# Scores of tiles 0 and 1 of a head pair in one PSUM buffer, and a new order of the units of a round

## The chip, the cores and the metric

The kernel runs on one core of one Trainium2 chip. The metric is the device time of one execution in microseconds (us). TensorE is called PE here, VectorE DVE, ScalarE ACT, GpSimd POOL, and SP is the engine whose queue issues the DMAs. PE writes its results to PSUM, from which DVE and ACT read them. Each engine works through its own instructions in the order of the program, and waits on semaphores for the others.

## The reference

Three stages follow each other; the change lies in the first and touches the start of the second.

```python
# 1. attention, 4 batches x 8 heads, 576 tokens, head size 64
scores = scale * np.matmul(q, k.transpose(0, 1, 3, 2))
mask = block_i >= block_j                       # blocks of 64 tokens
scores = np.where(mask, scores, -1000000000.0)
scores = scores - np.max(scores, axis=-1, keepdims=True)
attn = np.exp(scores)
attn = attn / (np.sum(attn, axis=-1, keepdims=True) + 1e-09)
out = np.matmul(attn, v)
# 2. x: 2304 tokens x 512, from out
h = x @ w_in                                    # 512 x 2048
g = np.where(h >= 1, h, np.where(h <= -1, 0.0, (h + 1) ** 2 / 4))
x = g @ w_out
# 3. a mixture of 8 experts on 32 slots, with softmax over tokens and over slots
```

## The kernel before

Two heads make a pair, so attention is 16 pairs (4 batches, 4 pairs each). A pair's 576 query rows are cut into tiles of 128 rows: tiles 0 to 3 for each of the two heads, and tile 4, which holds the last 64 rows of both heads. The mask is block-triangular, so tile i needs the first 128(i+1) keys.

The work of a pair is cut into units, named by two letters and a number. `sc`i computes the scores of tile i on PE: three passes of split fp32 for both heads, and for tiles 0 to 3 two small matmuls with `low` and `one` that add a large negative number where the mask is false. `mx`i takes row maxima on DVE into the tile `negm`, `ex`i the exponentials on ACT, with row sums as a by-product. `rs` makes reciprocals of the sums on DVE, and `no`i multiplies the rows with them on POOL. `pt`j turns chunks of the result on PE into PSUM, `pc`j copies them to SBUF (j = 1 and 3 on DVE, the others on ACT). `pa` and `pb` multiply with v on PE, for tiles 2 to 4 and for tiles 0 and 1. `xh` and `xl` split the result into two fp32r parts: `xh` on ACT and `xl` on DVE for tokens below 1024, one copy on DVE for later tokens. `kh`, `kl`, `qh` and `ql` split k and q, `lk`, `lq`, `lv` load, and `w0`, `w1`, `w2` prepare columns of `w_in`. `hm` is one block of the first product of stage 2 (12 matmuls, 128x512 each), `ha` (ACT) and `ho` (DVE) its bend; eleven such blocks are computed during attention, one in each of the rounds 9 to 19 (the table `EARLY`).

The order is written out by hand in the table `PLAN`. A round runs through it once. The digit ahead of a unit says how many pairs back the unit works: in round r, `3sc4` computes the scores of tile 4 of pair r-3, `2sc3` those of tile 3 of pair r-2, `5pa` the output of pair r-5. There are 22 rounds; rounds 5 to 17 have all units of attention. Every engine takes its share of the list in this order, and waits come from the tiles the units share.

PSUM is held by three pools: `psc` has two buffers of [128, 2, 512] fp32 (two banks each) for scores, `ptr` three of one bank for transposes, for `pb` and for the blocks `h`, and `ppv` one for `pa`. A unit that takes a buffer waits until the readers of its former content are done. In the kernel before, a round takes five score buffers, in the order sc4, sc1, sc0, sc3, sc2, from the two of `psc` in turn. So sc4 waits for ex3 of the round before, sc1 for ex2, sc0 for ex4, sc3 for ex1, and sc2 for ex0.

Stage 2 and 3 (`Moe.run`) follow after the last round, with their own order.

Of the kernel before, what the change touches and what calls it, by code (L numbers as in the profile page):

```python
# [7 lines left out]
F32 = mybir.dt.float32  # L8
# [6 lines left out]
P = 128  # L15
# [21 lines left out]
class Pair:  # L37
# [68 lines left out]

    def sc(self, i):
        e, nc = self.e, self.nc
        sc = self.scs[i] = e.psc.tile([P, 2, 512], F32, tag="sc", name=f"sc{self.nm}{i}")
        if i == 4:  # L110
            for k, (qa, ka) in enumerate(((0, 0), (0, 1), (1, 0))):
                for u in range(2):
                    nc.tensor.matmul(sc[:, u, 0:288], self.QD[:, qa], self.K[:, ka, 288 * u:288 * u + 288],
                                     start=(k == 0), stop=(k == 2))
            return
        n = 128 * (i + 1)
        rows = slice(0, 64), slice(64, 128)
        for k, (qa, ka) in enumerate(((0, 0), (0, 1), (1, 0))):
            for h, r in enumerate(rows):
                nc.tensor.matmul(sc[:, h, 0:n], self.Q[r, qa, 128 * i:128 * i + 128], self.K[r, ka, 0:n],  # L120
                                 start=(k == 0), stop=False)
        for h, r in enumerate(rows):
            nc.tensor.matmul(sc[:, h, n - 64:n], e.low[r], e.one[r], start=False, stop=True)  # L123

    def block(self, i):
        for u, b in enumerate(self.TILES[i]):
# [18 lines left out]
    def ex(self, i):  # L145
        for b, sc, pr in self.block(i):
            self.nc.scalar.activation(pr, sc, AF.Exp, bias=self.negm[:, b:b + 1], accum_out=self.sums[:, b:b + 1])  # L147
# [66 lines left out]
    def xl(self, a):  # L214
        for hi, lo, src in self.xparts(a):
# [4 lines left out]


PLAN = """
3sc4 4pc2 4no1 1ho0 4pt4 3ex2 2qh 4pt5 4pc5 3sc1 4pc4 3rs0 3mx4 3mx1 5pa
3ex4 3ex1 2ql 5xh1 5pb 2w2 5xh0 3rs2 3no2 4pc3 3no3 5xl1 3sc0 2sc3
3pt0 3mx0 3no4 5xl0 3pt1 1kh 1lq 2mx3 3lv 3ex0 3rs1 3pc1 4pt6 2sc2 0hm0
2mx2 1w1 3pc0 4pc6 2ex3 0ha0 1kl 0lk 3pt2 3pt3 3no0 0w0
"""
EARLY = {(9, 0): (0, 0), (10, 0): (0, 1), (11, 0): (0, 2), (12, 0): (0, 3), (13, 0): (1, 0), (14, 0): (0, 4),
         (15, 0): (1, 1), (16, 0): (0, 5), (17, 0): (1, 2), (18, 0): (0, 6), (19, 0): (1, 3)}
# [12 lines left out]
def attention(e, tc, nb=4, wl=(1, 1 + 2 * READY)):  # L242
    nc = tc.nc
    e.ENG = ENG

    def copy(eng, dst, src):
        if eng == "A":
            nc.scalar.copy(dst, src)  # L248
        elif eng == "D":
            nc.vector.tensor_copy(dst, src)  # L250
        else:
            nc.gpsimd.tensor_scalar(out=dst, in0=src, scalar1=1.0, scalar2=1.0, op0=ALU.mult, op1=ALU.mult)
    e.copy = copy
    e.eng = lambda c: nc.vector if c == "D" else nc.gpsimd

    e.QD, e.pr, e.v_ = [], [], []
    for i in range(2):
        e.QD.append(e.apool.tile([P, 2, P], F32R, tag=f"QD{i}", bufs=1, name=f"QD{i}"))
        z = (nc.gpsimd, nc.vector)[i]
        z.memset(e.QD[i][0:64, :, 64:P].bitcast(F32), 0.0)  # L260
        z.memset(e.QD[i][64:P, :, 0:64].bitcast(F32), 0.0)
        e.pr.append([e.apool.tile([P, P * (b // 2 + 1)], F32, tag=f"pr{i}{b}", bufs=1, name=f"pr{i}{b}")
                     for b in range(9)])
        z.memset(e.pr[i][8][:, 576:640], 0.0)
        e.v_.append(e.apool.tile([P, 5, 2, 64], F32, tag=f"natv{i}", bufs=1, name=f"vn{i}"))
        z.memset(e.v_[i][64:P, 4], 0.0)
    e.low = e.apool.tile([P, P], mybir.dt.bfloat16, tag="low", bufs=1, name="low")
    e.one = e.apool.tile([P, 64], mybir.dt.bfloat16, tag="one", bufs=1, name="one")
    nc.vector.memset(e.low, 0.0)
    nc.vector.memset(e.one, 1.0)  # L270
    for h in (0, 64):
        nc.vector.memset(e.low[h:h + 1, 0:64], -2.0 ** 127)
    pairs = [Pair(e, nc, b, p) for b in range(nb) for p in range(4)]
    n = len(pairs)
    plan = [(it - int(u[0]), u[1:]) for it in range(n + 6) for u in PLAN.split()]
    plan = [(i, u) for i, u in plan if ((i, int(u[2:])) in EARLY if u[0] == "h" and u[1] in "moa" else
                                        0 <= i < n if u[0] != "w" else wl[0] <= i < wl[1])]
    fill = [(int(u[0]), u[1:]) for u in FILL.split()]
    assert sorted(fill) == sorted(plan[:len(fill)])
    for i, u in fill + plan[len(fill):]:  # L280
        if u[0] == "h":
            e.moe.early(u[1], *EARLY[i, int(u[2:])])
        elif u[0] != "w":
            pairs[i].step(u)
        else:
            t, c = (i - wl[0]) // 2, slice((i - wl[0]) % 2 * 256, (i - wl[0]) % 2 * 256 + 256)
            if u == "w0" and c.start == 0:
                e.moe.w_raw(t)
            elif u == "w1":
                e.moe.w_mul(t, c)  # L290
                e.moe.w_bits(t, c)
            elif u == "w2":
                e.moe.w_parts(t, c, e.ENG["w"])
# [14 lines left out]
class Moe:  # L308
# [207 lines left out]
            self.g[b, f] = self.new([P, a, n], F32, f"g{b}_{f}")  # L516
        return self.g[b, f // a * a][:, f % a]

    def h_unit(self, b, f, mid=()):
        e, nc = self.e, self.nc  # L520
        n = self.BLK[b][1]
        w = self.w[f].rearrange("p a (k c) -> p a k c", k=4)
        ph = self.ph[b, f] = e.ptr.tile([P, 512], F32, tag="tr", name=f"h{b}_{f}")
        m = 0
        for kk in range(4):
            for wi, xi in ((0, 0), (0, 1), (1, 0)):
                nc.tensor.matmul(ph[:, 0:n], w[:, wi, kk], self.x(b, kk, xi)[:, 0:n], start=(m == 0), stop=(m == 11))  # L527
                m += 1
            if kk == 2:
                for fn, *a in mid:  # L530
                    getattr(self, fn)(*a)
        if f == 15:
            self.drop_x(b)
        if b == 4:
            self.drop(f"w{f}")
# [23 lines left out]
        nc.vector.tensor_tensor(out=g, in0=ph, in1=g, op=ALU.max)  # L559

    def early(self, what, b, f):
        if what == "m":
            self.h_unit(b, f)
        elif what == "a":
            self.bend_act(b, f, "D")
        else:
            self.bend_max(b, f, "D")
# [547 lines left out]
def tile_attention_mixtures(ctx, tc, q, k, v, w_in, w_out, phi, w1, w2a, w2b, outa, outb):  # L1115
# [33 lines left out]
    with tc.tile_pool(name="att", bufs=1, reuse_waits="tile") as e.apool:  # L1149
        attention(e, tc)  # L1150
        nc.sync.dma_start(e.phi, phi.rearrange("(k p) s -> p k s", p=P))
# [53 lines left out]
```

## Time and profile before

| | us |
|---|---|
| median of 3 runs | 538.68 |
| the three runs | 538.38, 538.68, 539.71 |
| the profiled execution | 538.28 |
| its span, first to last instruction | 536.5 |
| attention, rounds 0 to 20, within the span | about 5 to 209 |

In the profile's first part PE is busy 507.3 us (95% of the span), DVE 343.0 (64%), ACT 322.4 (60%) and POOL 201.6 (38%). These shares mix stages: during attention all four compute engines are busy most of the time, later PE works nearly alone and the end waits for weights from HBM. The engine rows that follow are read by their start times: the step from one row to the next on PE is what a unit cost there, its own work and its wait together, because the duration of a row of several matmuls covers gaps between them.

### The profile page before, as it was taken

Reading aid. Unit: us, or ns where it says so; the run is one execution under the profiler, and the core shown is the slowest. Engines: PE = TensorE matmul, PEld = TensorE weight load, DVE = VectorE, ACT = ScalarE, POOL = GpSimd, SP = SyncE. Lnnn points to the kernel's source line nnn. Section 1 sums busy time; section 2 is a strip of 40 time slices with the busy share of each in tenths; the row PEclk is TensorE's granted clock in tenths of the full one; section 3 lists DMA queues with packets and bytes.
Section 4 is the critical chain, followed back from the end, with each engine's and each line's share of the span. In section 5 each row is a group of like instructions: output and inputs, shape, how many; then the busy total and the mean of one; then the engine's idle time right before and its main releaser. Section 6 shows DMA issues by size and latency. Waiting matters only on the chain.

```text
span 536.5 us, 11758 instructions
## 1 busy us (share of the span) xinstructions
PE 507.3 (95%) x4538; PEld 384.6 (72%) x4538; DVE 343.0 (64%) x676; ACT 322.4 (60%) x732; POOL 201.6 (38%) x259
## 2 busy tenths in 40 slices
PE   6899999999999989999989999899999999989994
PEld 5687777777777767878767887788767888643463
DVE  7799998888886734888998645823464343531242
ACT  5899987777777642667768878634334545231131
POOL 4888986767775430555552212500001000010000
PEclk9799999999999999999999999999999999999997
DMA  4444454323221135412146875322176496799997
GB/s 154 118 125 124 117 129 121 101 85 110 73 72 51 28 106 188 160 46 78 41 137 230 281 265 168 121 93 83 25 258 227 158 374 217 256 339 399 410 413 303
DMA packets 42711, 91.01 MB, mean 170 GB/s; under 512 B 8736, under 2 KB 18080, under 8 KB 42656
## 3 DMA queue, kind: packets, MB, share of 16 engines
q1 hardware_dynamic: 42656, 90.26, 49.6%
q8 instruction: 36, 0.59, 0.5%
q14 instruction: 19, 0.16, 0.1%
HBM read 74.51 MB, written 14.68 MB: 166 GB/s over the span
## 4 chain that ended last, share of the span: by engine, by line
PE 65%; DVE 14%; ACT 7%; DMA 5%; issue 3%; POOL 0%; SPq 0%; DVEq 0%; ACTq 0%; POOLq 0%
PE h L527 32%; PE gn L581 5%; PE om L184 4%; PE sc L120 4%; PE lt L593 3%; PE s L631 3%; PE eh L987 3%; DMA ew<-in_w2b_dram 3%; ACT pr L147 2%; DVE nm L142 2%; DVE wab L455 2%; DVE g L559 2%; DVE g L558 2%; ACT g L545 1%; PE om L189 1%
## 5 line engine op out<-in xcount | busy, mean ns | idle before, releaser
L527 PE MATMUL h<-xh,w 128*128 128x512 f32 (+1 forms) x384 | 115.6, 368 | 0.0
L158 POOL TENSOR_SCALAR pr<-pr,sm 128x384 f32<-128x384 f32 (+2 forms) x144 | 86.3, 617 | 38.4 <-DVE sm L153 14.0
L527 PE MATMUL h<-xt,w 128*128 128x512 f32 x384 | 91.6, 395 | 1.7 <-ACT PT L248 1.7
L558 DVE SCALAR_TENSOR_TENSOR g<-g 128x512 f32<-128x512 f32 (+1 forms) x52 | 37.4, 720 | 82.3 <-ACT g L545 81.7
L147 ACT ACTIVATE pr<-sc,nm 128x512 f32<-128x512 f32 (+2 forms) x144 | 78.6, 559 | 11.9 <-DVE nm L142 8.6
L527 PEld LDWEIGHTS h<-xt,w 128*128 128x128 f32 x384 | 70.5, 188 | 18.6 <-ACT PT L248 2.1
L527 PEld LDWEIGHTS h<-xh,w 128*128 128x128 f32 x384 | 69.1, 189 | 13.7 <-issue 3.8
L545 ACT ACTIVATE g<-h,half 128x512 f32<-128x512 f32 (+1 forms) x52 | 32.4, 623 | 62.5 <-PE h L527 62.0
L527 PE MATMUL h<-xl,w 128*128 128x512 f32 (+1 forms) x192 | 68.2, 355 | 0.2 <-POOL xl L400 0.2
L559 DVE TENSOR_TENSOR g<-h,g 128x512 f32<-128x512 f32 (+1 forms) x80 | 50.8, 636 | 16.0 <-ACT g L550 14.0
L142 DVE TENSOR_REDUCE nm<-sc 128x2 f32<-128x1024 f32 (+1 forms) x64 | 51.8, 818 | 5.0 <-PE sc L123 4.4
L662 POOL TENSOR_TENSOR cn<-cn,cm 128x128 f32<-128x128 f32 (+1 forms) x5 | 1.9, 378 | 140.7 <-DVE cm L661 111.2
L120 PE MATMUL sc<-K,Q 64*128 64x512 f32 (+3 forms) x384 | 47.0, 360 | 3.6 <-ACT pr L147 3.2
L248 ACT COPY gn<-gn 128x1024 f32<-128x1024 f32 x35 | 35.3, 1009 | 16.0 <-PE gn L581 15.8
L527 PEld LDWEIGHTS h<-xl,w 128*128 128x128 f32 x192 | 36.4, 189 | 4.5 <-POOL xl L400 0.7
L120 PEld LDWEIGHTS sc<-K,Q 64*128 64x128 f32 x384 | 29.9, 194 | 13.3 <-ACT pr L147 6.7
L472 POOL TENSOR_TENSOR wab<-wab,w 128x256 f32<-128x256 f32 (+1 forms) x23 | 22.5, 980 | 40.9 <-ACT w L248 20.4
L465 POOL TENSOR_TENSOR wab<-wab 128x512 f32<-128x512 f32 x16 | 21.9, 1372 | 40.4 <-DVE wab L457 27.3
L581 PE MATMUL gn<-ident,g 128*128 128x128 f32 x280 | 36.5, 273 | 0.2 <-ACT gn L248 0.2
L581 PEld LDWEIGHTS gn<-ident,g 128*128 128x128 f32 x280 | 31.9, 140 | 5.4 <-issue 2.5
L455 DVE SCALAR_TENSOR_TENSOR wab<-wab 128x512 uint32<-128x512 uint32 (+1 forms) x39 | 28.5, 731 | 9.8 <-ACT wab L448 6.9
L547 ACT ACTIVATE g<-h,half 128x512 f32<-128x512 f32 x28 | 19.3, 688 | 22.5 <-PE h L527 20.1
(221 smaller groups left out, 901.7 us busy)
## 6 DMA issues: line engine op xcount, KB each, us to landing
ew<-in_w_dram SPq DMA_DIRECT2D x32, 512.0 KB, 6.3
raw<-in_w_in_dram SPq DMA_DIRECT2D x16, 512.0 KB, 5.3
raw<-in_w_out_dram SPq DMA_DIRECT2D x16, 512.0 KB, 4.1
ew<-in_w2a_dram SPq DMA_DIRECT2D x16, 510.0 KB, 8.8
ew<-in_w2b_dram SPq DMA_DIRECT2D x16, 344.0 KB, 6.8
kn<-in_k_dram SPq DMA_DIRECT2D x16, 288.0 KB, 3.9
qn<-in_q_dram SPq DMA_DIRECT2D x16, 288.0 KB, 3.2
vn<-in_v_dram SPq DMA_DIRECT2D x16, 256.0 KB, 3.3
```

The source lines that it names most:

```text
L120: nc.tensor.matmul(sc[:, h, 0:n], self.Q[r, qa, 128 * i:128 * i + 128], self.K[r, ka, 0:n], start=(k == 0), stop=False)
L142: nc.vector.tensor_reduce(out=self.negm[:, 2 * i:2 * i + 2], in_=self.scs[i][:, :, 0:128 * (i + 1)], axis=AX.X, op=ALU.max, negate=True)
L147: self.nc.scalar.activation(pr, sc, AF.Exp, bias=self.negm[:, b:b + 1], accum_out=self.sums[:, b:b + 1])
L158: self.nc.gpsimd.tensor_scalar(out=pr, in0=pr, scalar1=self.sums[:, b:b + 1], scalar2=1.0, op0=ALU.mult, op1=ALU.mult)
L248: nc.scalar.copy(dst, src)
L455: v.scalar_tensor_tensor(out=Au, in0=Au, scalar=3, in1=Bu, op0=ALU.logical_shift_left, op1=ALU.bitwise_or)
L472: p.tensor_tensor(out=A, in0=A, in1=w[:, 0].bitcast(F32), op=ALU.subtract)
L527: nc.tensor.matmul(ph[:, 0:n], w[:, wi, kk], self.x(b, kk, xi)[:, 0:n], start=(m == 0), stop=(m == 11))
L545: nc.scalar.activation(g, ph, AF.Relu, bias=e.half[:, 0:1], scale=0.5)
L558: nc.vector.scalar_tensor_tensor(out=g, in0=g, scalar=1.0, in1=g, op0=ALU.min, op1=ALU.mult)
L559: nc.vector.tensor_tensor(out=g, in0=ph, in1=g, op=ALU.max)
L581: nc.tensor.transpose(ps[:, j, i * P:(i + 1) * P], self.gt(b, f)[:, o:o + P], e.ident)
```

## The change

Three things change.

1. `sc(0)` takes no buffer of its own. Its scores go into columns 256 to 383 of the buffer of tile 1 (which uses columns 0 to 255), for both heads, so into the same two banks. A round takes four score buffers, in the order sc4, sc1, sc3, sc2.
2. The mask matmuls become units `mk0` to `mk3`, and the block `hm` becomes four units of three matmuls: `hm`, `hx`, `hy`, `hz`.
3. `PLAN` has another order, and other distances for some units.

```diff
     def sc(self, i):
         e, nc = self.e, self.nc
-        sc = self.scs[i] = e.psc.tile([P, 2, 512], F32, tag="sc", name=f"sc{self.nm}{i}")
+        if i == 0:
+            sc = self.scs[0] = self.scs[1][:, :, 256:384]
+        else:
+            sc = self.scs[i] = e.psc.tile([P, 2, 512], F32, tag="sc", name=f"sc{self.nm}{i}")
...
-        for h, r in enumerate(rows):
-            nc.tensor.matmul(sc[:, h, n - 64:n], e.low[r], e.one[r], start=False, stop=True)
+
+    def mk(self, i):
+        n = 128 * (i + 1)
+        for h, r in enumerate((slice(0, 64), slice(64, 128))):
+            self.nc.tensor.matmul(self.scs[i][:, h, n - 64:n], self.e.low[r], self.e.one[r], start=False, stop=True)
...
 PLAN = """
-3sc4 4pc2 4no1 1ho0 4pt4 3ex2 2qh 4pt5 4pc5 3sc1 4pc4 3rs0 3mx4 3mx1 5pa
-3ex4 3ex1 2ql 5xh1 5pb 2w2 5xh0 3rs2 3no2 4pc3 3no3 5xl1 3sc0 2sc3
...
+3sc4 4pt4 0w0 4pc4 3sc1 2w2 3mx4 1ha0 3ex4 3mk1 2ql 3mx1 5pa 1ho0 5pb
+5xh1 3sc0 3rs2 3mk0 2sc3 2mk3 5xh0 5xl1 3mx0 4pc5 3ex1 3lv 3no2 3no3 5xl0
...
+    def h_part(self, b, f, kk):
+        e, nc = self.e, self.nc
+        n = self.BLK[b][1]
+        if kk == 0:
+            self.ph[b, f] = e.ptr.tile([P, 512], F32, tag="tr", name=f"h{b}_{f}")
+        ph, w = self.ph[b, f], self.w[f].rearrange("p a (k c) -> p a k c", k=4)
+        for m, (wi, xi) in enumerate(((0, 0), (0, 1), (1, 0))):
+            nc.tensor.matmul(ph[:, 0:n], w[:, wi, kk], self.x(b, kk, xi)[:, 0:n], start=(kk + m == 0), stop=(kk + m == 5))
+
     def h_unit(self, b, f, mid=()):
...
         for kk in range(4):
-            for wi, xi in ((0, 0), (0, 1), (1, 0)):
-                nc.tensor.matmul(ph[:, 0:n], w[:, wi, kk], self.x(b, kk, xi)[:, 0:n], start=(m == 0), stop=(m == 11))
-                m += 1
+            self.h_part(b, f, kk)
...
     def early(self, what, b, f):
-        if what == "m":
-            self.h_unit(b, f)
+        if what in "mxyz":
+            self.h_part(b, f, "mxyz".index(what))
```

From `pa` of pair 14 (round 19) on, the instructions of PE are the same, in the same order, in both kernels; so are those of the other engines after attention.

**ACT in round 11, from the exponential of tile 4 on.** A name such as `sc1_31` is batch 1, pair 3, tile 1; `xt` is written by `xh`, `PT` by `pc`, `K` by `kh`. Before:

```order
L147 ACTIVATE pr18_191,sm1_3_1303<-sc1_34_1366,nm1_3_1302 128x576
L147 ACTIVATE pr12_185,sm1_3_1303<-sc1_31_1393,nm1_3_1302 128x256
L147 ACTIVATE pr13_186,sm1_3_1303<-sc1_31_1393,nm1_3_1302 128x256
L212 CAST xt11_145<-om1_1_1407 128x192
L212 CAST xt11_145<-ps1_1o_1434 128x256
L248 CAST K_2_1_1482<-kn2_1_1350 128x576
L147 ACTIVATE pr10_183,sm1_3_1303<-sc1_30_1451,nm1_3_1302 128x128
L147 ACTIVATE pr11_184,sm1_3_1303<-sc1_30_1451,nm1_3_1302 128x128
```

Now:

```order
L153 ACTIVATE pr18_191,sm1_3_1298<-sc1_34_1374,nm1_3_1297 128x576
L218 CAST xt11_145<-om1_1_1407 128x192
L218 CAST xt11_145<-ps1_1o_1428 128x256
L255 COPY PT1_2_1314<-ps1_2p5_1366 128x512
L153 ACTIVATE pr12_185,sm1_3_1298<-sc1_31_1387,nm1_3_1297 128x256
L153 ACTIVATE pr13_186,sm1_3_1298<-sc1_31_1387,nm1_3_1297 128x256
L255 CAST K_2_1_1472<-kn2_1_1335 128x576
L153 ACTIVATE pr10_183,sm1_3_1298<-sc1_31_1387,nm1_3_1297 128x128
L153 ACTIVATE pr11_184,sm1_3_1298<-sc1_31_1387,nm1_3_1297 128x128
```

The two exponentials of tile 1 (ex1) stood ahead of `xh1` and `xh0`; now they stand behind both and behind the copy `pc5`.

**DVE in the same round, from the maximum of tile 1 on.** Before:

```order
L142 TENSOR_REDUCE nm1_3_1302<-sc1_31_1393 128x2
L95 SCALAR_TENSOR_TENSOR Q_2_0_1385<-qn2_0_1300,Q_2_0_1385 128x576
L210 COPY xw20_148<-om1_1_1407 128x128
L152 TENSOR_SCALAR sm1_3_1303<-sm1_3_1303 128x1
L153 RECIPROCAL sm1_3_1303<-sm1_3_1303 128x1
L250 COPY PT1_2_1311<-ps1_2p3_1357 128x512
L218 TENSOR_TENSOR xt11_145<-om1_1_1407,xt11_145 128x192
L142 TENSOR_REDUCE nm1_3_1302<-sc1_30_1451 128x2
```

Now:

```order
L148 TENSOR_REDUCE nm1_3_1297<-sc1_31_1387 128x2
L567 SCALAR_TENSOR_TENSOR g0_0_1398<-g0_0_1398 128x512
L568 TENSOR_TENSOR g0_0_1398<-h0_0_1339,g0_0_1398 128x512
L216 COPY xw20_148<-om1_1_1407 128x128
L158 TENSOR_SCALAR sm1_3_1298<-sm1_3_1298 128x1
L159 RECIPROCAL sm1_3_1298<-sm1_3_1298 128x1
L224 TENSOR_TENSOR xt11_145<-om1_1_1407,xt11_145 128x192
L148 TENSOR_REDUCE nm1_3_1297<-sc1_31_1387 128x2
```

The last row is `mx0`: it now reads the tile `sc1_31`, and the bend `ho` (`g0_0`) stands between `mx1` and it, where the copy `pc3` and `ql` stood. In the program as built, ex1 waits for this `mx0`, and sc0 for `mx1`.

**PE at the end of round 11, from the block h on.** `p2`, `p3`, `p4`, `p5` are the transposes `pt`. Before:

```order
L527 MATMUL h0_1_1508<-xt02_142,w1_582 128x512 x3
L527 MATMUL h0_1_1508<-xt03_143,w1_582 128x512 x3
L166 MATMUL ps1_3p2_1536<-ident_116,pr18_191 128x128
...
L166 MATMUL ps1_3p3_1541<-ident_116,pr15_188 128x128
...
L113 MATMUL sc2_04_1548<-K_2_0_1298,QD0_165 128x288 x6
L166 MATMUL ps1_3p4_1560<-ident_116,pr10_183 128x128
...
L166 MATMUL ps1_3p5_1569<-ident_116,pr18_191 128x128
```

Now:

```order
L172 MATMUL ps1_3p2_1511<-ident_116,pr18_191 128x128
...
L533 MATMUL h0_1_1520<-xt00_140,w1_548 128x512 x3
L533 MATMUL h0_1_1520<-xt01_141,w1_548 128x512 x3
L533 MATMUL h0_1_1520<-xt02_142,w1_548 128x512 x3
L172 MATMUL ps1_3p5_1548<-ident_116,pr18_191 128x128
...
L533 MATMUL h0_1_1520<-xt03_143,w1_548 128x512 x3
L116 MATMUL sc2_04_1556<-K_2_0_1291,QD0_165 128x288 x6
L172 MATMUL ps1_3p4_1563<-ident_116,pr10_183 128x128
```

`pt5` stood behind `pt4` and took the buffer of h, so it waited for `ho`; now it stands between parts of h, and the buffer of h is next taken by `pt0` of the next round. The mask matmuls stand where they stood, directly behind the scores of their tile.

## Rows read from the trace of the kernel before

**Rows 1.** Busy us of each engine in two stretches of 20 us: PE, PEld, DVE, ACT, POOL
```profile
60.00:80.00 20.00, 19.48 (x211) 15.35 (x210) 18.62 (x43) 18.09 (x57) 17.51 (x27) 1.00 0.45 125
140.00:160.00 20.00, 19.75 (x175) 15.74 (x174) 17.14 (x38) 14.18 (x41) 14.36 (x22) 1.00 0.33 95
```

**Rows 2.** Timeline of PE: first matmuls of pa in rounds 5, 10 and 18
```profile
32.38 0.87 PE L184 MATMUL om<-PT,vn 128*64 128x256 f32 x6
...
85.77 1.08 PE L184 MATMUL om<-PT,vn 128*64 128x256 f32 x8
...
187.84 0.87 PE L184 MATMUL om<-PT,vn 128*64 128x256 f32 x6
```

**Rows 3.** Timeline of PE, round 8 (no block h): start us, us, what, [idle before]
```profile
65.00 0.55 PE L120 MATMUL sc<-K,Q 64*128 64x128 f32 x6
65.39 0.21 PE L123 MATMUL sc<-one,low 64*128 64x64 bf16 x2
...
67.48 0.79 PE L120 MATMUL sc<-K,Q 64*128 64x384 f32 x6
...
72.05 1.30 PE L184 MATMUL om<-PT,vn 128*64 128x256 f32 x10
```

**Rows 4.** Timeline of PE and its weight loads, rounds 13 and 14 (with h)
```profile
142.38 0.79 PE L120 MATMUL sc<-K,Q 64*128 64x384 f32 x6
...
143.18 3.06 PE L527 MATMUL h<-xt,w 128*128 128x512 f32 x12
146.08 1.03 PE L166 MATMUL ps_3p<-ident,pr 128*128 128x128 f32 x8
...
148.47 0.42 PEld L166 LDWEIGHTS ps_3p<-ident,pr 128*128 128x128 f32 x4 [0.36 <-DVE g L559]
...
152.55 0.55 PE L120 MATMUL sc<-K,Q 64*128 64x128 f32 x6
152.95 0.20 PE L123 MATMUL sc<-one,low 64*128 64x64 bf16 x2
...
155.17 0.47 PEld L120 LDWEIGHTS sc<-K,Q 64*128 64x128 f32 x6 [0.30 <-ACT pr L147]
```

**Rows 5.** Waits of PE's weight loads, 30 to 205 us: total us, times, longest
```profile
PEld h L527 <- ACT PT L248: 2.1, 2, 1.5
PEld ps_2p L166 <- DVE g L559: 1.7, 3, 1.0
PEld ps_0p L166 <- DVE g L559: 1.3, 2, 0.9
PEld ps_3p L166 <- DVE g L559: 1.3, 3, 0.5
...
PEld ps_1p L166 <- DVE g L559: 0.7, 2, 0.4
```

**Rows 6.** Timeline of ACT, round 8 (ex1, xh1, xh0, kh, ex0, pc5 with pc4)
```profile
63.94 0.47 ACT L147 ACTIVATE pr<-sc,nm 128x256 f32<-128x256 f32 x1
...
64.84 0.49 ACT L212 CAST xt<-om 128x256 fp32r<-128x256 f32 x2
65.20 0.41 ACT L212 CAST xt<-ps_3o 128x256 fp32r<-128x256 f32 x1
65.59 0.67 ACT L248 CAST K<-kn 128x576 fp32r<-128x576 f32 x1
66.29 0.37 ACT L147 ACTIVATE pr<-sc,nm 128x128 f32<-128x128 f32 x1
...
66.89 0.20 ACT L147 ACTIVATION_READ_ACCUMULATOR pr<-sc,nm 128x1 f32 x1
...
71.67 1.07 ACT L248 COPY PT<-ps_1p 128x512 f32<-128x512 f32 x2
```

**Rows 7.** Timeline of DVE, round 8 (mx0, then mx3)
```profile
65.84 0.41 DVE L142 TENSOR_REDUCE nm<-sc 128x2 f32<-128x256 f32 x1
...
66.50 1.21 DVE L142 TENSOR_REDUCE nm<-sc 128x2 f32<-128x1024 f32 x1
```

More of the change, by code (lines that the diff above doesn't have):

```diff
@@ L222 @@
 PLAN = """
-3sc4 4pc2 4no1 1ho0 4pt4 3ex2 2qh 4pt5 4pc5 3sc1 4pc4 3rs0 3mx4 3mx1 5pa
-3ex4 3ex1 2ql 5xh1 5pb 2w2 5xh0 3rs2 3no2 4pc3 3no3 5xl1 3sc0 2sc3
-3pt0 3mx0 3no4 5xl0 3pt1 1kh 1lq 2mx3 3lv 3ex0 3rs1 3pc1 4pt6 2sc2 0hm0
-2mx2 1w1 3pc0 4pc6 2ex3 0ha0 1kl 0lk 3pt2 3pt3 3no0 0w0
+3sc4 4pt4 0w0 4pc4 3sc1 2w2 3mx4 1ha0 3ex4 3mk1 2ql 3mx1 5pa 1ho0 5pb
+5xh1 3sc0 3rs2 3mk0 2sc3 2mk3 5xh0 5xl1 3mx0 4pc5 3ex1 3lv 3no2 3no3 5xl0
+3pt0 1kh 4pt6 3ex0 2mx3 3pt1 2sc2 3rs1 3pc0 4pc6 3no4 2mk2 3pc1 1kl 2mx2
+3no1 3pt3 3pt2 0lk 2ex3 0hm0 0hx0 3pc3 1w1 2ex2 0lq 3no0 3pc2 2rs0 0hy0
+1qh 3pt5 0hz0
 """
@@ L275, in attention @@
     plan = [(it - int(u[0]), u[1:]) for it in range(n + 6) for u in PLAN.split()]
-    plan = [(i, u) for i, u in plan if ((i, int(u[2:])) in EARLY if u[0] == "h" and u[1] in "moa" else
+    plan = [(i, u) for i, u in plan if ((i, int(u[2:])) in EARLY if u[0] == "h" and u[1] in "mxyzoa" else
                                         0 <= i < n if u[0] != "w" else wl[0] <= i < wl[1])]
@@ L517, in gt, with h_unit @@
         return self.g[b, f // a * a][:, f % a]
-    def h_unit(self, b, f, mid=()):
+    def h_part(self, b, f, kk):
         e, nc = self.e, self.nc
         n = self.BLK[b][1]
-        w = self.w[f].rearrange("p a (k c) -> p a k c", k=4)
-        ph = self.ph[b, f] = e.ptr.tile([P, 512], F32, tag="tr", name=f"h{b}_{f}")
-        m = 0
+        if kk == 0:
[3 more added lines that the diff above has]
+            nc.tensor.matmul(ph[:, 0:n], w[:, wi, kk], self.x(b, kk, xi)[:, 0:n], start=(kk + m == 0), stop=(kk + m == 5))
+    def h_unit(self, b, f, mid=()):
         for kk in range(4):
-            for wi, xi in ((0, 0), (0, 1), (1, 0)):
-                nc.tensor.matmul(ph[:, 0:n], w[:, wi, kk], self.x(b, kk, xi)[:, 0:n], start=(m == 0), stop=(m == 11))
-                m += 1
+            self.h_part(b, f, kk)
             if kk == 2:
```

## The prediction

> **What bounds the kernel now.** I read the page's shares first, then a table of busy time by stretch, then the timelines of single rounds, engine by engine. Attention is the only stage that the change touches; behind it every instruction is the same, so a gain or loss in the rounds moves the end by the same amount, as far as I can see. In the rounds, PE is busy 19.48 of 20 us in a stretch without blocks h and 19.75 in one with them [rows 1]. In the first stretch DVE has 18.62 and ACT 18.09 beside it, so three engines share the bound; in the second PE leads alone, DVE has 17.14 and ACT 14.18. So a round without h is bound by PE and DVE together, a round with h by PE.
>
> Next, how long a round is, from one `pa` to the next. Rounds 5 to 8 (no h): from 32.38 to 72.05, 39.67/4 = 9.92 us [rows 2, 3]. Rounds 10 to 17 (with h): from 85.77 to 187.84, 102.07/8 = 12.76 us [rows 2]. Round 9 is longer, 85.77 - 72.05 = 13.72.
>
> A busy PE is not a working PE: its waits must be taken out. In the round from sc2 at 142.38 to sc2 at 155.17, 12.79 us, two waits are seen: 0.36 us in which the transposes `pt5` wait for the bend `ho` (the releaser is DVE, line 559), and a wait of sc2 for an ACT exponential, ex0 [rows 4]. The second is small: sc0 starts at 152.55, and in round 8, where sc2 waits for nothing long, the step from sc0 to sc2 is 67.48 - 65.00 = 2.48 [rows 3]; here it is 2.62, so 0.14. PE's own work with h is 12.79 - 0.36 - 0.14 = **12.29 us**. The block h takes 146.08 - 143.18 = 2.90 of it, so without h it is **9.39**.
>
> **What the change removes.** The wait of `pt5` for `ho`: 1.7 + 1.3 + 1.3 + 0.7 = 5.0 us over ten waits, and twice a wait of h for a copy `pc`, 2.1 us in all [rows 5]. In the new order `pt0` takes the buffer of h. It comes 1.35 us and more after `pb`, and `ho` comes right behind mx1, ahead of `pb`'s end, so I expect none of that 5.0 to come back. That is the gain on offer, some 7 us. Taking one score tile out of five from the two buffers also removes the wait of sc0 for ex4, which cost nothing visible.
>
> The mask units and the four parts of h are the same matmuls. The masks stand directly behind their scores, as before; of h only the last part is moved behind `pt5`. Both cost nothing: the work is PE's own and already in the 12.29. If a change of operand between parts cost something, it would be two changes a round.
>
> **What it adds.** Let T be the start of sc0, right behind `pb`. PE then has sc0, sc3, `pt0`, `pt6` and `pt1` to do, and wants to start sc2 at T + 2.48. Before, sc2 needed ex0, and ex0 needed `mx0`; ex1 and, on ACT, everything else of tile 1 was done before T. Now sc2 still needs ex0 (it takes the buffer that tiles 0 and 1 share), but ex1 stands behind `mx0`. The chain, by rows of before:
> - The masks of sc0 end at 152.95 + 0.20, so T + 0.60 [rows 4].
> - `mx0` on DVE takes 0.41: T + 1.01 [rows 7].
> - ex1 takes 64.84 - 63.94 = 0.90: T + 1.91 [rows 6].
> - `kh` takes 0.67: T + 2.58 [rows 6].
> - ex0 takes 66.89 + 0.20 - 66.29 = 0.80: T + 3.38 [rows 6].
>
> So sc2 starts 3.38 - 2.48 = **0.90 us late**, in every round, and nothing but PE's own later units stands behind it. For pairs whose `xh` is on ACT (rounds 5 to 12) ACT's queue gives a little more: `xh0` starts at T + 0.20 and ends at T + 0.59, `pc5` takes half of 1.07, so ex1 starts at T + 1.12 instead of 1.01, and sc2 is **1.01 us** late [rows 6]. Signals between engines are not counted, so both are lower bounds. Why ex1 waits for `mx0` at all: in the program as built the wait is there. No stretch of before has two score tiles in one buffer.
>
> The Trainium skill, page "PSUM — Partial Sum Buffer", section "PSUM bank collisions raise a hardware error", says that two engines must not be in one bank at the same time, reads against reads included, and tells authors to guard by bank and not by address. By that rule the two tiles in one bank must take turns, and the order mx1, sc0, mx0, ex1 is forced; by address alone ex1 could run before T in rounds 13 to 17, sc2 would not be late there, and the sum below would be 4.5 us less, 540.9. No run here shows a collision.
>
> What is late next: in a round without h, DVE. Its reciprocals `rs1` need ex0 and stand behind mx3. mx3 can end at about T + 2.7 (the masks of sc3 end near T + 1.45, 1.21 for mx3 [rows 7]), ex0 at T + 3.4 to 3.5: DVE, which works 9.4 to 10 us of such a round, gets a new idle stretch of about 0.8.
>
> **The sum**, against the profiled run's own 538.28 us (its span is 536.5; the median of the runs is 0.40 above it):
> - Rounds 10 to 12: 12.29 + 1.01 = 13.30 against 12.76, 3 x 0.54 = 1.6. Rounds 13 to 17: 12.29 + 0.90 = 13.19, 5 x 0.43 = 2.2. The removed waits are in this already, since 12.29 holds none.
> - Round 9: 13.30 against 13.72, -0.4.
> - Rounds 5 to 8: by PE 9.39 + 1.01 = 10.40 (+0.48 each), by DVE up to 10.1 + 0.8 = 10.9 (+1.0). I take the value between, 10.6: 4 x 0.7 = 2.8.
> - Rounds 3 and 4 have the same chain but no `pa`; PE is not full there. Between 0 and 1 each; I take 0.5: 1.0.
> - Rounds 18 and 19 have no sc2, and lose only the wait for `ho`: -0.5.
>
> Together 1.6 + 2.2 - 0.4 + 2.8 + 1.0 - 0.5 = **+6.7 us**. 538.28 + 6.7 = 545.0 for a profiled run, **545.4** as a median. With the low ends (0.48 in rounds 5 to 8, 0 in 3 and 4) it is +4.8, so 543.5; with the high ones (DVE's 1.0, 1.0 in rounds 3 and 4, 0.8 in each of the rounds 10 to 17 for signals and a late bend, nothing back in round 9) 2 + 4 + 6.4 - 0.5 = +11.9, so 550.6.
>
> **The rivals.**
> - *Faster: the chain has slack that I don't see.* If ex1 is done before T after all, or sc2's place behind `pt1` gives it the time, all of the 7.1 us of waits goes [rows 5], and the time is 538.7 - 7.1 = 531.6. For it: PE is the bound with h, and the new order plainly aims `ho` and `pc` away from its waits. Against: the step from sc0 to sc2 is only 2.48, and ex1 plus ex0 alone are 1.70 on ACT. It decides from the point at which ex0 ends before T + 2.5.
> - *No change: both work, at a smaller size.* If the late start is about 0.45 instead of 0.9 (`kh` slipping ahead, shorter exponentials), thirteen rounds pay 13 x 0.45 = 5.9 and get back most of the 7.1: 537.5 to 540.
> - *Slower by more: DVE becomes the bound in the rounds with h as well.* `ho` stands between mx1 and `mx0`, and its two instructions are 1.4 us; if mx4 comes late, `ho` pushes `mx0` past T + 1.01, and each 0.1 us there is 0.1 on PE. At 0.6 more in each of eleven rounds, 552.
>
> **How the numbers follow.** My forecast (541.5 to 550.6) has 0.66, the larger loss 0.10, no change 0.10, the gain 0.14. A measurement tells 0.3% (1.6 us) from no change, so slower has 0.76, same 0.10 and faster 0.14. The range leaves out most of the gain and the end of the larger loss: 537 to 552.
>
> **What would show it.** In the profile after, the step from sc0 to sc2 in a round should be about 3.4 to 3.6 instead of 2.5, with ACT's exponentials named as the releaser of sc2; the eight rounds with h should take 13.2 to 13.5; ex1 should start right behind `mx0`, after `pb`; no wait of a transpose for line 559's successor should be left. I am wrong if ex1 starts before `pb` ends, if sc2 starts within 2.6 us of sc0, or if the time after attention's end is not that of before.

## The result, and the profile after

The changed kernel takes **546.56 us** (median of 4 runs, 545.56 to 547.45), beside 538.78 us for the kernel before in the same session (4 runs). The ratio is 1.0146, 95% interval 1.0126 to 1.0166: slower by 1.5%, where 545.4 us was forecast. Its profiled execution took 547.04 us with a span of 544.9, against 538.28 and 536.5 before.

Rounds are measured from one first matmul of `pa` to the next, as in the prediction. Those of rounds 5, 9, 10, 13 and 18 in the kernel after:

```profile
34.94 1.73 PE L190 MATMUL om<-PT,vn 128*64 128x256 f32 x16
...
78.14 1.73 PE L190 MATMUL om<-PT,vn 128*64 128x256 f32 x16
...
91.50 1.73 PE L190 MATMUL om<-PT,vn 128*64 128x256 f32 x16
...
131.00 1.73 PE L190 MATMUL om<-PT,vn 128*64 128x256 f32 x16
...
197.16 1.74 PE L190 MATMUL om<-PT,vn 128*64 128x256 f32 x16
```

| stretch | before, us | after, us | difference | predicted |
|---|---|---|---|---|
| start, to the first `pa` (round 5) | 32.38 | 34.94 | +2.56 | +1.0 |
| rounds 5 to 8, each | 9.71, 9.88, 10.13, 9.95 | 10.66, 10.84, 10.86, 10.84 | +3.53 | +2.8 |
| round 9 | 13.72 | 13.36 | -0.36 | -0.4 |
| rounds 10 to 12, each | 12.64, 13.16, 12.56 | 13.17, 13.17, 13.16 | +1.14 | +1.6 |
| rounds 13 to 17, each | 12.72 to 12.79 | 13.39, 13.38, 13.40, 13.40, 12.59 | +2.45 | +2.2 |
| rounds 18 and 19 | 11.83, 6.52 | 10.92, 5.91 | -1.52 | -0.5 |
| together | | | **+7.80** | **+6.7** |

Busy time in the two stretches of [rows 1], for the kernel after (columns: window, length, then PE, PEld, DVE, ACT, POOL, granted clock, DMA share, GB/s):

```profile
60.00:80.00 20.00, 18.11 (x194) 14.16 (x194) 17.88 (x39) 17.20 (x54) 15.87 (x25) 1.00 0.44 123
140.00:160.00 20.00, 18.90 (x189) 15.42 (x189) 17.38 (x35) 13.93 (x38) 14.59 (x21) 1.00 0.18 51
```

PE had 19.48 and 19.75 there. In both stretches it now stands idle for more than a microsecond, and no other engine is full in its place (DVE, the next, has 17.88 and 17.38). This is what a wait looks like in a table of busy time: the leading engine is less busy, and none is full.

The timeline of PE shows where. Round 8, which answers to [rows 3]:

```profile
70.38 0.55 PE L123 MATMUL sc<-K,Q 64*128 64x128 f32 x6
70.77 0.21 PE L129 MATMUL sc<-one,low 64*128 64x64 bf16 x2
...
73.82 0.79 PE L123 MATMUL sc<-K,Q 64*128 64x384 f32 x6 [0.89 <-ACT pr L153]
```

From sc0 to sc2 it is 73.82 - 70.38 = 3.44 us, where [rows 3] have 2.48; 0.89 of it is a wait for an ACT exponential. Round 15, one of those in which DVE makes `xh0`, on PE:

```profile
160.67 0.55 PE L123 MATMUL sc<-K,Q 64*128 64x128 f32 x6
161.06 0.20 PE L129 MATMUL sc<-one,low 64*128 64x64 bf16 x2
...
164.33 0.79 PE L123 MATMUL sc<-K,Q 64*128 64x384 f32 x6 [1.11 <-ACT pr L153]
```

The same microseconds on ACT (ex1, `kh`, ex0):

```profile
161.99 0.47 ACT L153 ACTIVATE pr<-sc,nm 128x256 f32<-128x256 f32 x1 [2.33 <-DVE nm L148]
...
162.90 0.67 ACT L255 CAST K<-kn 128x576 fp32r<-128x576 f32 x1
163.46 0.38 ACT L153 ACTIVATE pr<-sc,nm 128x128 f32<-128x128 f32 x1
```

And on DVE (`xh0`, then `mx0`):

```profile
161.22 0.41 DVE L216 COPY xw<-ps_2o 128x256 f32<-128x256 f32 x1
161.54 0.41 DVE L148 TENSOR_REDUCE nm<-sc 128x2 f32<-128x256 f32 x1
```

This is the predicted chain, link by link: the masks of sc0, then `mx0` (161.54), ex1 right behind it (161.99, after 2.33 us of idle time), `kh` (162.90), ex0 (163.46), and sc2. Here it is 0.22 longer than in round 8, since `mx0` stands behind DVE's copy `xh0` (161.22), and that copy in its turn behind the bend `ho`, in a stretch of DVE without idle time that begins with mx4 at 156.85.

From 30 to 205 us, the list of PE's waits reads (total us, times, longest):

```profile
PE sc L123 <- ACT pr L153: 11.8, 13, 1.1
```

No transpose waits for the bend `ho` any more. Line 568, which is line 559 of before, is named only ahead of score matmuls: their weight loads wait behind it seven times, 0.2 us at most and 1.2 in all. On DVE the reciprocals `rs1` have the idle stretch that was forecast (round 8):

```profile
71.84 1.23 DVE L148 TENSOR_REDUCE nm<-sc 128x2 f32<-128x1024 f32 x1
73.80 0.77 DVE L158 TENSOR_SCALAR sm<-sm 128x4 f32<-128x4 f32 x1 [0.73 <-ACT pr L153]
```

### The profile page after: what moved, and what is told of

The parts are those of the page before. It is cut to its first block, busy times and chain, and to the rows that moved or that the text cites. A ratio compares the mean times of both kernels' runs of the same rounds, so it can differ in the third digit from the quotient of the medians.

```text
span 544.9 us, 11721 instructions
## 1 busy us (share of the span) xinstructions
PE 506.5 (93%) x4538; PEld 384.8 (71%) x4538; DVE 351.8 (65%) x676; ACT 321.2 (59%) x732; POOL 201.9 (37%) x259
## 4 chain that ended last, share of the span: by engine, by line
PE 67%; DVE 11%; DMA 10%; ACT 7%; issue 3%; POOL 1%; SPq 0%; DVEq 0%; ACTq 0%; POOLq 0%
PE h L533 32%; PE sc L123 6%; PE gn L590 5%; DMA ew<-in_w2a_dram 5%; PE lt L602 3%; PE om L190 3%; PE s L640 3%; ACT pr L153 3%; DMA ew<-in_w2b_dram 2%; DVE nm L148 2%; PE ps_1p L172 2%; PE ps_3p L172 2%; PE ps_2p L172 2%; DVE sm L158 2%; PE sc L116 1%
## 5 line engine op out<-in xcount | busy, mean ns | idle before, releaser
L164 POOL TENSOR_SCALAR pr<-pr,sm 128x384 f32<-128x384 f32 (+2 forms) x144 | 88.5, 631 | 26.5 <-DVE sm L159 19.7
L533 PE MATMUL h<-xt,w 128*128 128x512 f32 x384 | 94.1, 397 | 0.0
L567 DVE SCALAR_TENSOR_TENSOR g<-g 128x512 f32<-128x512 f32 (+1 forms) x52 | 38.6, 743 | 74.6 <-ACT g L554 74.0
```

The costliest lines, as they stand in the source:

```text
L164: self.nc.gpsimd.tensor_scalar(out=pr, in0=pr, scalar1=self.sums[:, b:b + 1], scalar2=1.0, op0=ALU.mult, op1=ALU.mult)
L567: nc.vector.scalar_tensor_tensor(out=g, in0=g, scalar=1.0, in1=g, op0=ALU.min, op1=ALU.mult)
```

## The experiments

Each experiment but the last changes one thing in the kernel after, or in the one before where it says so; the last joins two orders. In a session of four kernels the kernel before took 537.78 us (13 runs), in one of three kernels 538.16 us (7 runs).

**ex1 ahead of `pa`.** Without anything else moved, ex1 is issued right behind mx1, so that it no longer follows `mx0`.

```diff
-... 3mk1 2ql 3mx1 5pa 1ho0 5pb
-5xh1 3sc0 3rs2 3mk0 2sc3 2mk3 5xh0 5xl1 3mx0 4pc5 3ex1 3lv ...
+... 3mk1 2ql 3mx1 3ex1 5pa 1ho0 5pb
+5xh1 3sc0 3rs2 3mk0 2sc3 2mk3 5xh0 5xl1 3mx0 4pc5 3lv ...
```

> The changed kernel with one unit moved: ex1 stands right behind mx1, ahead of pa, pb and sc0. Theory (one buffer for tiles 0 and 1, and ex1 behind sc0 in the order, so ex1 waits for mx0): ex1 then waits for mx1 alone and is done before pb ends; the step from sc0 to sc2 falls from 3.44 to 3.66 us back to about 2.5, rounds 5 to 8 from 10.8 to about 9.9, rounds 10 to 16 from 13.2 to 13.4 to about 12.4; 546.6 - 12 = about 535. Rival (ACT's and DVE's new order as such, with pc5 and kh between ex1 and ex0 and the reciprocals behind them): nothing of that is changed here, so 545 to 546.

539.90 us, ratio 1.0047 (1.0029 to 1.0065). Rounds 10 to 17 take 12.21 or 12.22 us, all eight: PE works through them without a wait (12.29 had been worked out for this from the kernel before). So the place of ex1 behind `mx0` is the whole loss of these rounds, 0.95 to 1.19 us in each (0.37 in round 17, which has no `kh`). But the total missed: rounds 5 to 8 stayed at 10.60 to 10.90, and the first `pa` came at 36.0, later still. Rounds 5 to 8 have another limit, and the timelines show where the new waits stand. PE at sc0 of round 7:

```profile
61.63 0.55 PE L123 MATMUL sc<-K,Q 64*128 64x128 f32 x6 [1.18 <-ACT pr L153]
```

DVE right behind it, at `xl1`:

```profile
61.99 0.56 DVE L224 TENSOR_TENSOR xt<-om,xt 128x256 fp32r<-128x256 f32 x2 [1.21 <-ACT xt L218]
```

Now sc0 waits for ex1, whose buffer it shares, and `xl1` on DVE waits for `xh1`, which ACT makes behind ex1. DVE has one idle stretch a round in either version: 0.73 ahead of `rs1` after the change, 1.21 ahead of `xl1` here.

**A buffer of its own for sc0**, in the changed order.

```diff
-        if i == 0:
-            sc = self.scs[0] = self.scs[1][:, :, 256:384]
-        else:
-            sc = self.scs[i] = e.psc.tile([P, 2, 512], F32, tag="sc", name=f"sc{self.nm}{i}")
+        sc = self.scs[i] = e.psc.tile([P, 2, 512], F32, tag="sc", name=f"sc{self.nm}{i}")
```

> The changed kernel with its order, but sc0 takes a buffer of its own again (five takes a round). Theory: ex1 waits for mx1 alone. In rounds 13 to 17 (no xh on ACT) ex1 is then done before pb and sc2 is not late: 12.3 to 12.4 us instead of 13.39. In rounds 5 to 12 sc3 now takes the buffer of tile 1, and ex1 stands behind xh0 and pc5 on ACT: sc3 starts about 1.6 us late, so these rounds are some 0.6 longer than in the changed kernel. In all 544 to 547. Rival (the order alone is to blame): rounds 13 to 17 stay at 13.4.

546.10 us, 1.016 (1.0131 to 1.0188). Two kinds of rounds come apart. Rounds 13 to 17 fall to 12.21, as with ex1 moved: unshared, ex1 does not wait for `mx0`, and sc2 is in time. Rounds 9 to 12 rise to 13.76, since sc3 now takes the buffer that ex1 reads, and ex1 stands behind `xh0` and `pc5` on ACT:

```profile
97.58 0.55 PE L120 MATMUL sc<-K,Q 64*128 64x128 f32 x6
97.97 0.20 PE L126 MATMUL sc<-one,low 64*128 64x64 bf16 x2
99.53 0.96 PE L120 MATMUL sc<-K,Q 64*128 64x512 f32 x6 [1.36 <-ACT pr L150]
```

The changed order therefore leans on the shared buffer in these rounds and suffers from it in the later ones. The start (35.49) and rounds 5 to 8 (12.53, then 10.96 or 10.97) are no better than with sharing, so the changed order has a loss there with either buffer. For rounds 5 to 8 this says less than it seems, because the same 1.36 us of wait at sc3 stands in them too, which sharing does not have. Round 5 with its 12.53 is a case by itself: the granted clock was 0.86 in it, and 1.00 in the rounds that follow.

**Sharing alone**, in the order of before.

```diff
-        sc = self.scs[i] = e.psc.tile([P, 2, 512], F32, tag="sc", name=f"sc{self.nm}{i}")
+        if i == 0:
+            sc = self.scs[0] = self.scs[1][:, :, 256:384]
+        else:
+            sc = self.scs[i] = e.psc.tile([P, 2, 512], F32, tag="sc", name=f"sc{self.nm}{i}")
```

> The kernel before with its order, but sc0 writes into columns 256 to 383 of the buffer of tile 1. Theory: ex1 stands ahead of sc0 in this order, so sc0 waits for ex1, which was done by then; rounds 5 to 17 as before, rounds 3 and 4 up to 1 us longer each: 538.5 to 541. Rival (sharing a buffer costs by itself): 544 to 548.

539.57 us (10 runs), 1.0031 (1.0018 to 1.0045). Rounds are as before (12.64 to 12.79 with h, 9.70 to 10.25 without), and the first `pa` is at 33.33 instead of 32.38: in rounds 3 and 4 sc0 waits 2.43 and 2.62 us for an exponential, where it waited 1.25 and 1.58 with a buffer of its own. Sharing by itself, in the old order, costs about 1 us at the start and nothing that shows in the later rounds, where ex1 is long done.

**`kh` behind ex0**, one link out of the chain.

```diff
-3pt0 1kh 4pt6 3ex0 2mx3 ...
+3pt0 4pt6 3ex0 1kh 2mx3 ...
```

> The changed kernel with one unit moved: kh stands behind ex0 on ACT instead of between ex1 and ex0. Theory (the chain mx0, ex1, kh, ex0, sc2 sets the round): sc2 starts 0.56 us earlier in each of the rounds 3 to 16, so 546.6 - 14 x 0.56 = 538.7; if DVE takes over in rounds without h, 541. Rival (PE waits for something else): within 0.5 of 546.6.

544.64 us (542.11 to 546.63), 1.0131 (1.009 to 1.0173). The wait of sc2 falls from 0.89 to 0.32, by `kh`'s 0.57, so the chain is real. The rounds with h gain less, 13.17 to 12.88 and 13.39 to 12.91, since the copies that the next transposes wait for now stand behind `kh`:

```profile
109.49 0.79 PE L123 MATMUL sc<-K,Q 64*128 64x384 f32 x6 [0.32 <-ACT pr L153]
110.54 1.09 PE L172 MATMUL ps_0p<-ident,pr 128*128 128x128 f32 x8 [0.21 <-ACT PT L255]
```

The forecast of the time (538.7 to 541) missed. The first `pa` comes 1.0 us sooner (33.93), but rounds 5 to 8 do not fall at all: they take 11.00 to 11.02 us, 0.16 longer than rounds 6 to 8 after, with three new waits of PE's transposes beside the 0.32, for that copy (0.22) and for products of POOL (0.26 and 0.20).

**Less work for DVE.** Two of the four instructions of the weight bits are left out; the order stays that of after.

```diff
         v.tensor_scalar(out=Bu, in0=hi, scalar1=0x80000000, ...)
-        v.scalar_tensor_tensor(out=Au, in0=Au, scalar=3, in1=Bu, ...)
-        v.tensor_scalar(out=Bu, in0=Au, scalar1=0xff800000, ...)
         v.scalar_tensor_tensor(out=B, in0=lo, scalar=2.0 ** -52, in1=B, ...)
```

> The changed kernel with two of the four instructions of the weight bits left out (the shift with its or, and the mask of the exponent; the weights come out wrong), so that DVE has some 0.75 us less to do in every round that turns weights (to round 17), and nothing else moves. Theory: in rounds 3 to 8 DVE is a closed loop (it waits 0.74 us for ex0 at rs1, and else has work all the way round: 9.77 of 10.84 us), so rounds 5 to 8 fall from 10.84 to 10.3 or less, where PE's own work with sc2's lateness (9.4 + 0.9) takes over, and the start comes 0.7 to 2 us earlier; rounds 10 to 17 stay at 13.2 to 13.4. Rival: sc2's late release through ex1, kh and ex0 sets rounds 5 to 8 by itself as it does the later ones; then they stay at 10.8 and the start too.

539.67 us (one run). This is not the worth of DVE's work in attention: of the 7.0 us by which the span is shorter, 2.9 lie up to the last `pa` and 4.1 behind it, where weights are turned too and the same two instructions are gone. The first `pa` comes at 32.0, 2.94 us sooner, in two parts. sc0 of round 4 comes 1.81 us sooner (23.95 instead of 25.76), a little over 0.75 for each of the two turns of weight bits ahead of it: it waits for mx1, and DVE works without a stop from 17.07 up to that mx1 in the kernel after, so up to there DVE sets the pace. The other 1.13 us lie between this sc0 and `pa`, where PE waits for nothing in either kernel, but is granted 0.79 of its clock here and 0.68 after.

Rounds 13 to 16, which the theory left at 13.4, fell to 13.17 to 13.19: the first instruction of `ho` is shorter here, so `xh0` and `mx0` behind it come sooner behind `pb`. In round 15, in the kernel after and here:

```profile
158.81 1.05 DVE L567 SCALAR_TENSOR_TENSOR g<-g 128x512 f32<-128x512 f32 x1
...
154.86 0.68 DVE L565 SCALAR_TENSOR_TENSOR g<-g 128x512 f32<-128x512 f32 x1
```

Why it is shorter was not traced. Rounds 10 to 12 stayed at 13.17, as the theory has it. Rounds 6 to 8 fell only from 10.85 to 10.67, not to 10.3, and round 5, which has 10.66 in the kernel after, did not fall at all. The chain of waits of a round without h shows what holds 10.67. In the kernel after it had gone through DVE from `rs1` by way of the bits, `mx4` and `ql` to `mx1`, and from there through PE and ex0; now it goes through PE and ex0 alone (start, us, what):

```profile
57.61 0.05 PE sc L129 x2
57.65 0.59 PE ps_0p L172 x4
58.24 0.11 PE ps_3p L172
58.35 0.45 PE ps_0p L172 x4
58.80 0.01 issue
58.81 0.16 ACT pr L153
58.96 0.10 issue
59.07 0.56 ACT pr L153 x3
59.63 0.04 issue
59.67 0.79 PE sc L123 x3
60.46 0.05 PE sc L129
60.51 1.66 PE ps_0p L172 x12
62.17 0.80 PE sc L116 x6
62.97 0.49 PE ps_0p L172 x4
```

PE is full but for the 0.87 between 58.80 and 59.67. So PE's own work without h is 10.67 - 0.87 = 9.80 us, and not the 9.39 of the prediction. (Round 5 of before, in which the profile shows no wait of PE, took 9.71.) Both limits, DVE at 10.85 and PE with the late sc2 at 10.67, lie almost together. Part of the 0.4 can be seen: twelve transposes in a row take 1.66 and four more 0.49, 2.15 in all; where pieces of h stand between them, they take 1.90 (chain of waits in the version with ex1 ahead, rounds 14 and 15):

```profile
150.91 0.44 PE ps_3p L172 x4
...
152.85 0.44 PE ps_3p L172 x4
...
160.02 1.02 PE ps_0p L172 x8
```

The other 0.15 or so was not traced further.

**`mx0` ahead.** The masks and the maximum of tile 0 right behind sc0, ahead of DVE's `xh0` and `xl1`.

```diff
-5xh1 3sc0 3rs2 3mk0 2sc3 2mk3 5xh0 5xl1 3mx0 4pc5 3ex1 ...
+5xh1 3sc0 3mk0 3mx0 3rs2 2sc3 2mk3 5xh0 5xl1 4pc5 3ex1 ...
```

> The changed kernel with the mask and the maximum of tile 0 put straight behind sc0, ahead of rs2, xh0 and xl1 on DVE. Theory: in rounds 13 to 17 mx0 stands behind DVE's copy xh0, which makes sc2 1.10 instead of 0.89 us late, so these rounds go from 13.39 to 13.17, the value of rounds 10 to 12, and the later ones gain nothing else; rounds 5 to 8 may lose a little, since xl1 comes later. About 545.5 us. Rival: mx0 ahead of xl1 frees ex1 up to 0.5 us sooner in every round, the rounds go to 12.8 and the time to 541; or the masks, now ahead of sc3 on PE, cost as much as they bring and the rounds stay at 13.4.

545.02 us (one run). Rounds 13 to 16 take 13.16 or 13.17, exactly the value of rounds 10 to 12, with 0.89 us of wait at sc2; the other rounds do not move (10.67 to 10.87, 13.16, 13.17), and the first `pa` comes 0.67 us sooner (34.27). `mx0` behind the copy `xh0` was the 0.22 us; with less work for DVE the same 0.22 went although `xh0` stayed ahead, so either remedy is enough.

**Both orders in one kernel.** Up to round 8 the order and the buffers of before; from round 9 on the changed order with ex1 right behind mx1. Round 9 also runs the units that the old order does one round later.

```diff
-        if i == 0:
+        if i == 0 and 4 * self.b + self.p + 3 >= S:
...
+S = 9
...
-    plan = [(it - int(u[0]), u[1:]) for it in range(n + 6) for u in PLAN.split()]
+    plan = [(it - int(u[0]), u[1:]) for it in range(n + 6) for u in (FIRST if it < S else TURN if it == S else PLAN).split()]
```

> Rounds up to 8 in the order of the kernel before, with a buffer for tile 0's scores of its own; from round 9 on the changed order with ex1 straight behind mx1 and the shared buffer; round 9 also runs the units that stand a round later in the old order. Theory: the loss lies in the rounds up to 8 (first pa at 32.4, rounds of 9.7 to 10.1 by the old order against 34.9 and 10.85) and in ex1's place behind mx0 (rounds 10 to 17 of 12.21 against 13.2 to 13.4), and the two are apart: first pa 32.4, rounds 5 to 8 as before, round 9 13.5 to 14.5, rounds 10 to 17 12.21, rounds 18 and 19 10 and 5.9; 531 to 533 us, ratio 0.987 to 0.990. Rival: the old order's lead in the first rounds is only borrowed, and round 9 gives it back with its doubled units (4 us or more); then 536 or more.

**532.64 us** (532.27 to 533.26), ratio 0.9901 (0.9885 to 0.9918): 1.0% faster than the kernel before, and so than the one after. First `pa` at 32.37; rounds 5 to 8 take 10.13 to 10.26; round 9 13.03; rounds 10 to 17 12.21 or 12.22; rounds 18 and 19 10.08 and 5.91. The two losses are apart, and round 9 with its doubled units is shorter than in either kernel (13.72 and 13.36). PE in the stretches of [rows 1]:

```profile
60.00:80.00 20.00, 18.38 (x207) 14.61 (x206) 18.07 (x42) 17.57 (x55) 17.25 (x25) 1.00 0.54 155
140.00:160.00 20.00, 20.00 (x180) 16.38 (x179) 17.15 (x38) 15.07 (x43) 15.53 (x24) 1.00 0.30 83
```

In the second stretch PE is busy all of the 20 us. In rounds 5 to 8 this kernel is some 0.27 us a round above the one before, with the same order. PE's waits at sc4 for an ACT exponential are part of it, 1.6 us in these four rounds against 0.8; why they are longer was not found out.

## Why the prediction was right, and where it was off

**The main mechanism held.** sc2 starts 3.44 us behind sc0 (3.66 in rounds 13 to 16) where 3.4 to 3.6 was forecast; ex1 starts right behind `mx0` and after `pb`; the transposes' waits for `ho` are gone. Each link was confirmed by taking it away: ex1 moved (rounds of 12.21), no sharing (12.21 in rounds 13 to 17), `kh` moved (0.57 less), `mx0` moved (0.22 less). PE's own work with h, forecast as 12.29, is 12.21.

**Rounds 10 to 12** (+1.14, forecast +1.6): the 0.11 us that ACT's queue was to add (1.01 late instead of 0.90, with `xh0` and `pc5` ahead of ex1) did not come: sc2 waits 0.89, as if `mx0` alone set ex1. `pc5` stands ahead of ex1 there, but is done in time.

**Rounds 13 to 17** (+2.45, forecast +2.2): the term missed that in these rounds DVE makes `xh0`, which stands behind `ho` and ahead of `mx0`: 1.11 late instead of 0.90. It missed in the other direction that round 17 has no `kh`, as no pair is left to load: 12.59.

**Rounds 5 to 8** (+3.53, forecast +2.8): two bounds were written down, 10.40 by PE and up to 10.9 by DVE, and a value between them was taken. When two limits both apply the larger one counts. DVE's was written as 9.4 to 10.1 us of work and 0.8 of idle time, so 10.2 to 10.9, and its upper end is what came: 10.66, then 10.84 to 10.86. DVE works 9.77 of the 10.84 us and waits 0.73 once a round, at `rs1`, for an ex0 that hangs on DVE's own `mx0`; the chain of waits leads through DVE. This bound was real, but little above the next: with 0.75 us less work for DVE a round fell by 0.18. The bound by PE was too low in the prediction, 10.67 instead of 10.40, since PE's own work without h was taken as the work with h less the block h (9.39), and the transposes cost more when no h stands between them.

**The start** (+2.56, forecast +1.0) is the worst of the terms. It was sized as the same late sc2 in rounds where PE has room. The rows show two things in its place. 1.97 us of the loss are there when sc0 of round 4 starts (25.76, before 23.79), and DVE leads up to there. The order makes it wait in new places: sc0, for one, waits for mx1, whose buffer it shares,

```profile
14.53 0.90 PE L123 MATMUL sc<-K,Q 64*128 64x128 f32 x6 [1.97 <-DVE sm L158]
...
25.76 0.91 PE L123 MATMUL sc<-K,Q 64*128 64x128 f32 x6 [3.01 <-DVE sm L158]
```

(the profile names the DVE instruction behind mx1). The prediction had this wait in its order (mx1, sc0, `mx0`, ex1), but priced ex1's alone. The other 0.59 us lie between this sc0 and the first `pa`, and there the clock differs. The same 64 matmuls, in the kernel before, in the one after and with less work for DVE (columns as above, the granted clock third from the end):

```profile
23.79:32.38 8.59, 8.27 (x64) 6.86 (x64) 7.53 (x17) 7.37 (x23) 7.12 (x12) 0.80 0.40 113
25.76:34.94 9.18, 9.18 (x64) 7.55 (x64) 6.35 (x14) 6.79 (x23) 6.09 (x11) 0.68 0.52 162
23.95:32.00 8.05, 8.05 (x64) 6.77 (x64) 6.35 (x14) 6.81 (x23) 6.86 (x12) 0.79 0.62 184
```

PE is busy all of the time in the second and third; the second has more of its time at the lower of the two levels (1.2 GHz) and takes 1.13 us longer. Over all nine profiles the granted clock from 7 to 33 us is 0.74 in the four whose first `pa` comes latest (the kernel after, ex1 moved, a buffer of its own, `mx0` moved: 34.27 to 36.00) and 0.80 in the five others (32.0 to 33.93). The prediction priced no clock. Which comes first, the longer waits or the lower clock, these runs do not separate. With a buffer of its own the start was no shorter (35.49), and sharing alone, in the old order, cost 0.95: so most of the loss belongs to the new order, but which of its moves makes it was not shown.

**Rounds 18 and 19** (-1.52, forecast -0.5): the 2.1 us in which h waited for a copy `pc` [rows 5] lie in these two rounds of before. The prediction listed them as removed, but booked only the wait for `ho` here.

Too low in three terms (1.56 + 0.73 + 0.25) and too high in two (0.46 + 1.02), the sum came out 1.1 us short. The remaining 0.6 of the longer span lies behind attention. The kernel after has 3.3 us there at a granted clock of 0.50 (277.5 to 280.8), where the one before has 1.00; but sharing alone and both orders, which have no such stretch, take longer still from the last `pa` to the end (331.2 and 331.3 us, against 330.9 after and 330.3 before), so the clock does not settle it. Of the prediction's own figures one has no source: the forecast's lower end, 541.5, where its low ends add up to 543.5.

Of the rivals, "faster" fell because ex0 does end after T + 2.5. It was not far off, though: with one unit moved the rounds with h did give back their waits. "No change" by a late start of 0.45 was near the version with `kh` moved (0.32 + 0.21 in a round): its eight rounds 10 to 17 took 12.86 us on average, against 12.76 before, and the rest of its 1.3% lies mainly in the rounds up to 8 (5.9 us). "DVE also bounds the rounds with h" fell by its size, not by its kind: `ho`, with `xh0` behind it, did push `mx0`, but by 0.22 in four rounds and not by 0.6 in eleven. The rule of the Trainium skill on guarding by bank (page "PSUM — Partial Sum Buffer", section "PSUM bank collisions raise a hardware error") pointed the right way: the tiles take turns, and by address alone 540.9 had been worked out. The turns are waits of the program as built; what two engines in one bank at once would do, no run here shows.

## What to carry to other kernels

Two tiles in one buffer take turns: before sharing, write down for each reader which unit of the other tile must now go first, in both directions (here ex1 behind `mx0`, and sc0 behind mx1), and see whether the first tile's readers can be issued before the second tile's scores (with h that took away the whole loss of the rounds; without h sc0 then waited 1.18 us for ex1). An order that is best where one engine leads (here PE, with h) can be the worse one where another does (here DVE, without h), so measure by stage and, where a table sets the order, give each stage its own. Where a step has two bounds, forecast the larger one, and look whether an engine's only wait in a round hangs on its own work, as DVE's did here. Before a difference is put down to waits, compare the granted clock of the two stretches.

## What was not expected of the hardware

After the same idle stretch of 1.61 us in round 18, PE kept its clock in one kernel and lost it in two others. Two stretches, one with the wait and one from its end, in the kernel after (window, length, PE, PEld, DVE, ACT, POOL, granted clock, DMA share, GB/s):

```profile
200.40:203.40 3.00, 1.39 (x15) 1.11 (x13) 1.14 (x5) 2.24 (x10) 0.75 (x1) 1.00 0.56 139
203.40:206.40 3.00, 3.00 (x17) 2.58 (x18) 1.16 (x2) 0.70 (x2) 1.62 (x4) 1.00 0.90 329
```

The same two in the kernel with less work for DVE:

```profile
196.00:199.00 3.00, 1.39 (x16) 1.11 (x13) 1.15 (x5) 2.32 (x10) 0.77 (x2) 1.00 0.60 146
199.00:202.00 3.00, 3.00 (x12) 2.71 (x13) 1.08 (x2) 0.62 (x2) 1.60 (x4) 0.52 0.90 322
```

In both, PE had been busy 1.39 of the last 3 us. In the second the granted clock then fell to 0.52, the lower level of 1.2 GHz, for some 3 us, and the round took 12.50 instead of 10.92 us. The profiled run with `kh` moved fell in the same way (0.51, 12.54 us). Of three profiles with this idle stretch two lost the clock; where the wait in this round was shorter (0.71 to 0.78 with ex1 moved, with a buffer of its own and with both orders) or in two pieces (0.50 and 0.93 with `mx0` moved), none did. A longer wait is not needed, though: with a buffer of its own the clock fell in round 5, after 1.36 us of wait at sc3, and did not in the rounds that follow, with the same wait; that round took 1.56 us more. So about 1.6 us of difference between two kernels, or between runs of one, can be the clock after one wait, and single figures above hold it (539.67, the highest of 542.11 to 546.63, and the 12.53 of round 5). What decides it these runs do not show.
